# Fused relu-squared attention and GeGLU block: the last output tile on whole rows, one activation table, and a re-tuned instruction plan

## The chip, the cores and the metric

The kernel runs on 1 core of a Trainium2 chip. The metric is the device time of one execution in microseconds (us), lower is better. The kernel before takes 436.75 us, the median of 4 runs from 435.96 to 437.55.

## The reference

```python
def _attn_ref(q, k, v):                      # q, k, v: (8, 12, 448, 64) float32
    scores = (1 / np.sqrt(64)) * np.matmul(q, k.transpose(0, 1, 3, 2))
    attn = np.maximum(scores, 0.0) ** 2 / 448
    return np.matmul(attn, v)
...
x = attn_out.transpose(0, 2, 1, 3).reshape(3584, 768)
def _moe_ref(x, w_gate, w_val, w_out):       # (768, 1536), (768, 1536), (1536, 768)
    g = x @ w_gate
    gelu = 0.5 * g * (1.0 + erf(g / sqrt(2)))
    return (gelu * (x @ w_val)) @ w_out      # (3584, 768) float32
```

There is no softmax: the attention weight is the squared relu of a score. The output of attention, tokens by 768, goes straight through a gated feed-forward block.

## The kernel before, in words

All matrix products are in bf16 with 64x64 operands. TensorE's 128x128 array is used as four 64x64 quarters, two row halves ("lower" and "upper", after the input partitions 0 to 63 and 64 to 127) by two column halves; four matmuls on different quarters run side by side. A sum over 128 inputs is therefore made as two matmuls into the same PSUM bank: first the lower half's whole accumulation, then the upper half's. Two lists of operations, PE0 for the lower half and PE1 for the upper, are merged into TensorE's one instruction stream.

For each batch (b = 0 to 7) the work is:

- q, k and v are loaded by DMAs that GpSimd (POOL) issues, with a cast to bf16 (`load_qk`, `load_v`). Batches 0 and 1 come in three groups of four heads; batch 2 in one piece; from batch 3 on each load waits for a feed-forward step of the batch two before (`[done]` in `add_gate_value`), for batch 3 starting at step fc = 3 of batch 1.
- q and k are transposed into `qkT`. Batches 0 and 1 do it on TensorE (`add_transposes`: 28 small matmuls for a group, copied out by VectorE, L324); later batches copy q and k on VectorE into `qkr` (L249) and use seven DMA transposes from SyncE (L257).
- Scores (`add_scores`): 21 units a batch, each into one of two PSUM tiles `sp`; ScalarE takes the relu (`rl`, L367), VectorE squares it (`attnT`, L373).
- Values (`add_values`): the squares of a pair of heads times v give 128 rows of `xT` (VectorE copies and scales them, L422).
- Gate and value (`add_gate_value`): 12 steps fc; a gate accumulation goes through gelu on ScalarE (`gel`, L460), a value accumulation is multiplied with it on VectorE (`uT`, L465).
- Output (`add_out`): a tile of 128 tokens in two column groups of 384; each group is 12 lower and then 12 upper steps of two matmuls; ScalarE copies it out (`osb`, L512), and after the second group SyncE stores two times 64 rows (L517).

PSUM banks for everything but the scores come from a ring of four (`new_bank`, tag F).

The order of instructions on every engine is fixed when the program is built, by a planner. `work` holds every accumulation with a due time; `lower` and `upper` sort PE's operations; `run_plan` then plays the operations through with a cost and a lag for each and emits them as they would start. PE0 and POOL are queues in a fixed order; PE1, ACT, DVE and SP are pools from which the operation that can start first is taken. A load's arrival is played as its bytes over a rate (400 GB/s of float32) plus 2 us. Where PE would idle in the first 45 us of the plan, `fill` puts in dummy matmuls on zeros (`warm`, 128x128, 256 columns), which write nothing that is read. Each engine works its list strictly in order, so an operation that the plan places too early holds up all that is behind it.

Of the kernel before, what the change touches and what calls it, by code (L numbers as in the profile page):

```python
# [88 lines left out]
def kernel(  # L89
# [10 lines left out]
    nc = tc.nc  # L100
    f32 = mybir.dt.float32
# [42 lines left out]
    warm = const.tile([128, 512], bf16)  # L144
    nc.vector.memset(warm[:, :], 0.0)

    ctx.enter_context(tc.manual_schedule())

    HALF = (slice(0, P), slice(P, 2 * P))
# [20 lines left out]
    w12_op, wo_op, head_op = {}, {}, {}  # L170
    qk16, v16 = {}, {}

    def load(nbytes, emit, deps=(), cost=0.7):
        def paced():
            ins = emit()
            for d in deps:
                tc.add_manual_dep(ins.ins, d.ins.name, SYNC, reason="pace")

        op = Op("POOL", cost, paced, deps)
        arrivals[op] = nbytes / 400e3  # L180
        POOL.append(op)
        return op

# [14 lines left out]
    def load_qk(b, i, h0, h1, deps=()):  # L198

        src = (q, k)[i]  # L200

        def tile_of():
            if b not in qk16:
                qk16[b] = qkv.tile([128, H * S // P * D], bf16, name="qk16", tag="qk16")
            return qk16[b][HALF[i], :]

        op = load(4 * (h1 - h0) * S * D, lambda: nc.gpsimd.dma_start(  # L207
            tile_of().rearrange("p (h x) -> p h x", h=H)[:, h0:h1, :],
            src[b, h0:h1].rearrange("h (p c) d -> p h (c d)", c=SC)), deps)
        for pr in range(h0 // 2, h1 // 2):  # L210
            head_op[b, pr, i] = op

    def load_v(b, h0, h1, deps=()):

        for i in range(2):
            def emit(i=i):
                if b not in v16:
                    v16[b] = qkv.tile([128, H, VC, D], bf16, name="v16", tag="v16")
                c0 = i * (SC - VC)
                return nc.gpsimd.dma_start(  # L220
                    v16[b][HALF[i], h0:h1, :, :],
                    v[b, h0:h1].rearrange("h (p c) d -> p h c d", c=SC)[:, :, c0:c0 + VC, :])
            op = load(4 * (h1 - h0) * VC * P * D, emit, deps)
            for pr in range(h0 // 2, h1 // 2):
                head_op[b, pr, 2 + i] = op

# [81 lines left out]
    def add_transposes(at, b, m):  # L308

        box = {}  # L310

        def emit(i, pr, c):
            if i not in box:
                box[i] = new_bank(t_op[b, m, i], [128, 2, SC * P], bf16)
            t = box[i]
            src = qk16[b].rearrange("p (h c d) -> p h c d", c=SC, d=D)
            for j in range(2):
                nc.tensor.transpose(  # L318
                    t[HALF[j], pr, c * P:(c + 1) * P], src[HALF[i], 2 * (2 * m + pr) + j, c, :],
                    ident[HALF[i], HALF[i]], tile_position=(P * i, P * j))  # L320

        def emit_copy(i):
            dst = qkT_tile(b).rearrange("d (c r) x -> d r c x", c=SC)
            nc.vector.tensor_copy(  # L324
                dst[:, 2 * m:2 * m + 2, :, HALF[i]],
                box[i].rearrange("d r (c p) -> d r c p", c=SC))

        ops = [[], []]
        for i in range(2):
            have = [head_op[b, 2 * m, i], head_op[b, 2 * m + 1, i], *ring_dep()]  # L330
            for pr in range(2):
                for c in range(SC):
                    ops[i].append(Op(f"PE{i}", 0.05, lambda i=i, pr=pr, c=c: emit(i, pr, c),
                                     have, lag=0.2))
            t_op[b, m, i] = Op("DVE", 0.63, lambda i=i: emit_copy(i),
                               [ops[i][-1], last_s.get(b - 2)], lag=0.1, prio=1)
            DVE.append(t_op[b, m, i])
            ring.append(t_op[b, m, i])
        both(at, zip(*ops), GS / 2 if b else 0.0)

    def add_scores(at, b, u):
# [35 lines left out]
        else:  # L377
# [2 lines left out]
        ops = [[Op(f"PE{j}", 0.095 if tail else 0.189, lambda j=j, pr=pr: emit(j, pr), have, lag=0.24)  # L380
                for pr in prs] for j in range(2)]
        last_s[b] = ops[1][-1]
        relu = Op("ACT", 0.92, emit_relu, [ops[0][-1], ops[1][-1], *sq_list[-4:-3]], lag=0.06, prio=2)
        n_a = len(sq_list)
        sq = Op("DVE", 0.64, emit_sq, [relu, *att_free[n_a - 12:n_a - 11]] if n_a >= 12 else [relu],
                lag=0.1, prio=2)
        units.append(relu)
        sq_list.append(sq)
        att_free.append(None)
        for pr in prs:  # L390
            sq_op.setdefault((b, pr), []).append((sq, n_a))
        ACT.append(relu)
        DVE.append(sq)
        both(at, zip(*ops))

    sq_list, att_free = [], []

    def add_values(at, b, pr):
        box = {}
# [21 lines left out]
        def emit_copy():  # L421
            nc.vector.tensor_scalar_mul(xT[b][:, pr, :], box[0][:, 0:S], scalar1=out_scale)  # L422

        sqs = sq_op[b, pr]
        have = [*(s for s, _ in sqs), head_op[b, pr, 2], head_op[b, pr, 3]]
        order = ([0, 1, 2, 3], [3, 0, 1, 2])
        ops = [[Op(f"PE{i}", 0.189 if w < VC - 1 else 0.095, lambda i=i, w=w: emit(i, w),
                   [*have, *(ring_dep() if i == 0 else ())], lag=0.24) for w in order[i]]
               for i in range(2)]
        o_op[b, pr] = ops[1][-1]  # L430
        for _, n_a in sqs:
            att_free[n_a] = o_op[b, pr]
        x_op[b, pr] = Op("DVE", 0.63, emit_copy, [o_op[b, pr]], lag=0.1, prio=1)
        DVE.append(x_op[b, pr])
        ring.append(x_op[b, pr])
        then(at, 0.0, *ops, x_op[b, pr])
# [5 lines left out]
    def add_gate_value(at, b, fc, g):  # L442
# [28 lines left out]
        if g == 0:  # L471
            done = gel_op[b, fc] = Op("ACT", 0.55, emit_gelu, [ops[1][-1]], lag=0.06, prio=0)
            ACT.append(done)
        else:
            done = u_op[b, fc] = Op("DVE", 0.63, emit_mult, [gel_op[b, fc], ops[1][-1]],
                                    lag=0.1, prio=0)
            DVE.append(done)
            n = fc - (3 if b == 1 else 0)
            if b + 2 < B and b and 0 <= n < 9:
                h0 = 4 * (n % 3)  # L480
                if n < 6:
                    load_qk(b + 2, n // 3, h0, h0 + 4, [done])
                else:
                    load_v(b + 2, h0, h0 + 4, [done])
                if n == 5:
                    add_dma_transposes(b + 2)
        ring.append(done)
        then(at, GS, *ops, done)

    def add_out(at, t, g):  # L490

# [22 lines left out]
        def emit_store(j):  # L514
            b, c = chunks[j]
            rows = out[b * S:(b + 1) * S, :].rearrange("(p c) d -> c p d", c=SC)
            nc.sync.dma_start(rows[c], osb[t][HALF[j], :])  # L517

        ops = [[Op(f"PE{r}", RS, lambda r=r, fc=fc: emit(r, fc),
                   [wo_op[fc // WOG], *(u_op[b, fc] for b, _ in chunks),  # L520
                    *(ring_dep() if r == 0 and fc == 0 else ())], lag=0.24)
# [36 lines left out]
    for b in range(B):  # L558
        starts.append(at)
        for fc in range(FC):  # L560
            for g in range(2):
                work.append((at, 5, add_gate_value, (b, fc, g)))
                at += G

        while 2 * tile_no + 1 < SC * (b + 1) - (2 if b < B - 1 else 0):
            for g in range(NG):
                work.append((at, 5, add_out, (tile_no, g)))
                at += R
            tile_no += 1
    starts.append(at)  # L570
    LEAD = 6.0
    for b in range(B):
# [2 lines left out]
        elif b == 1:  # L575
            lo, hi = 0.0, starts[1] - LEAD
        elif b == 2:
            lo, hi = starts[1] + 6.0, starts[2] - LEAD
        else:
            lo, hi = starts[b - 1] - LEAD, starts[b] - LEAD  # L580
        step = (hi - lo) / NU
# [90 lines left out]
```

## Time and profile before

| what | value |
|---|---|
| median of 4 runs | 436.75 us (435.96 to 437.55) |
| the profiled execution | 436.18 us, its span 434.3 us |
| TensorE busy | 420.8 us, 97% |
| ScalarE, VectorE busy | 225.3 us (52%), 205.5 us (47%) |
| first real matmul | 4.98 us |
| first gate matmul | 31.43 us |
| last matmul ends, last copy ends, span ends | 429.3, 429.83, 434.3 us |
| activation tables loaded | two: at 0.74 us and at 34.27 us, 1.28 us each |
| dummy fill matmuls | 32 |
| stores | 56, issued by SyncE, 192 KB each |

A busy share of 97% says little by itself here, because a matmul on one quarter of the array counts as busy just like four on all quarters. What can be read is where TensorE's stream stands still, and what it stands for. A line of a timeline gives the start, the duration, the engine (PE for matmuls, PEld for their weight loads, DVE for VectorE, ACT for ScalarE, POOL for GpSimd, SP for SyncE), the source line, the operation, output<-inputs, and, in brackets, how long the engine idled before it and what ended that.

### The profile page before, as it was taken

What the parts mean: (1) busy time and instruction counts of PE and PEld (TensorE: products, weight loads), DVE (VectorE), ACT (ScalarE), POOL (GpSimd) and SP (SyncE); (2) the same over time, 40 slices, a digit from 0 to 9 for tenths busy, and PEclk for the clock granted to TensorE, in tenths of its full rate; (3) what the DMA queues carried; (4) which work ended last, traced back from release to release, by engine and by line L of the source; (5) the groups of instructions that cost most, each with busy time, mean ns of one, the idle gap of its engine ahead of it and who ended that gap; (6) DMA issues with size and microseconds to landing.
All of it is one profiled execution on the core that took longest, in us unless ns stands there. A gap on an engine that the chain in (4) does not pass through costs nothing.

```text
span 434.3 us, 19901 instructions
## 1 busy us (share of the span) xinstructions
PE 420.8 (97%) x9224; PEld 365.5 (84%) x9224; DVE 205.5 (47%) x367; ACT 225.3 (52%) x322; POOL 68.4 (16%) x110
## 2 busy tenths in 40 slices
PE   6999989999999999999999999999999999999995
PEld 3557968879988778999999878999999878977894
DVE  1885666156733565355733566345733555212200
ACT  1966654266655565465556555555546565322221
POOL 6654500012300230012200231012200000000000
PEclk8899999999999999999999999999999999999998
DMA  8999999916993679356943669346942100120034
GB/s 109 197 198 198 203 209 180 174 27 85 119 180 77 87 93 154 77 88 91 157 73 94 90 85 157 96 82 88 149 92 77 40 3 2 49 66 3 3 83 102
DMA packets 75154, 44.92 MB, mean 103 GB/s; under 512 B 36160, under 2 KB 71488, under 8 KB 75072
## 3 DMA queue, kind: packets, MB, share of 16 engines
q0 software_dynamic: 36992, 24.39, 41.3%
q1 hardware_dynamic: 38080, 19.28, 24.6%
q8 instruction: 72, 1.18, 1.1%
q14 instruction: 10, 0.08, 0.1%
HBM read 48.76 MB, written 11.01 MB: 138 GB/s over the span
## 4 chain that ended last, share of the span: by engine, by line
PE 83%; DMA 12%; POOL 2%; ACT 1%; issue 1%; DVE 0%; POOLq 0%; ACTq 0%; DVEq 0%
PE ff L155 77%; DMA qk<-in_k_dram 12%; PE sp L155 6%; POOL qk L207 1%; ACT rl L367 1%; POOL v L220 0%; ACT osb L512 0%; POOL wv L188 0%; PE ff L318 0%; DVE qkr L249 0%; DVE attnT L373 0%; DVE uT L465 0%; POOL ident masks.py:199 0%; POOL ident masks.py:197 0%; POOLq masks.py:199 0%
## 5 line engine op out<-in xcount | busy, mean ns | idle before, releaser
L155 PE MATMUL ff<-xT,wg 64*64 64x448 bf16 x2304 | 217.9, 349 | 0.2 <-issue 0.2
L155 PE MATMUL ff<-xT,wv 64*64 64x448 bf16 x2304 | 217.7, 349 | 0.0
L367 ACT ACTIVATE rl<-sp 128x896 bf16<-128x896 f32 x168 | 152.0, 923 | 107.3 <-PE sp L155 82.0
L155 PE MATMUL ff<-wo,uT 64*64 64x384 bf16 x2688 | 150.4, 323 | 1.0 <-DVE uT L465 1.0
L155 PEld LDWEIGHTS <-wg 64*64 64x64 bf16 x2304 | 130.2, 107 | 14.8 <-issue 0.6
L155 PEld LDWEIGHTS <-wv 64*64 64x64 bf16 x2304 | 130.2, 107 | 13.7 <-issue 1.0
L373 DVE TENSOR_TENSOR attnT<-rl 128x896 bf16<-128x896 bf16 x168 | 103.8, 623 | 78.9 <-ACT rl L367 77.8
L155 PEld LDWEIGHTS <-uT 64*64 64x64 bf16 x2688 | 126.2, 107 | 6.3 <-DVE uT L465 1.3
L155 PE MATMUL sp<-qkT 64*64 64x448 bf16 (+1 forms) x768 | 108.0, 333 | 2.5 <-ACT rl L367 1.1
L465 DVE TENSOR_TENSOR uT<-gel,ff 128x448 bf16<-128x448 bf16 x96 | 59.5, 620 | 79.3 <-PE ff L155 71.2
L155 PE MATMUL ff<-attnT,v 64*64 64x448 bf16 (+1 forms) x768 | 86.0, 326 | 0.0
L460 ACT ACTIVATE gel<-ff 128x448 bf16<-128x448 f32 x96 | 52.1, 543 | 51.2 <-PE ff L155 50.6
L155 PEld LDWEIGHTS <-qkT 64*64 64x64 bf16 x768 | 45.3, 107 | 12.7 <-issue 7.5
L512 ACT COPY osb<-ff 128x384 f32<-128x384 f32 x56 | 26.7, 476 | 45.3 <-PE ff L155 45.1
L155 PEld LDWEIGHTS <-v 64*64 64x64 bf16 x768 | 46.7, 107 | 3.5 <-issue 0.2
L422 DVE TENSOR_SCALAR xT<-ff 128x448 bf16<-128x448 f32 x48 | 29.9, 623 | 34.6 <-PE ff L155 33.5
L207 POOL DMA_DIRECT2D qk<-in_q_dram x22 | 13.9, 631 | 162.7 <-DVE uT L465 161.3
L220 POOL DMA_DIRECT2D v<-in_v_dram x44 | 27.5, 631 | 29.0 <-DVE uT L465 14.5
L207 POOL DMA_DIRECT2D qk<-in_k_dram x22 | 13.7, 622 | 33.6 <-DVE uT L465 32.5
L318 PEld LDWEIGHTS <-qk 64*64 64x64 bf16 x336 | 9.0, 116 | 6.7 <-DMA qk<-in_k_dram 4.4
L249 DVE COPY qkr<-qk 128x768 bf16<-128x768 bf16 x42 | 13.6, 363 | 1.7 <-DMA qk<-in_k_dram 1.7
L318 PE MATMUL ff<-ident,qk 64*64 64x64 bf16 x336 | 10.4, 201 | 3.7 <-DMA qk<-in_k_dram 2.7
(19 smaller groups left out, 38.9 us busy)
## 6 DMA issues: line engine op xcount, KB each, us to landing
out_dram<-osb SPq DMA_DIRECT2D x56, 192.0 KB, 2.7
v<-in_v_dram POOLq DMA_DIRECT2D x42, 128.0 KB, 4.9
qk<-in_q_dram POOLq DMA_DIRECT2D x21, 224.0 KB, 3.7
qk<-in_k_dram POOLq DMA_DIRECT2D x21, 224.0 KB, 3.8
wg<-in_moe_w_gate_dram POOLq DMA_DIRECT2D x6, 384.0 KB, 11.3
wv<-in_moe_w_val_dram POOLq DMA_DIRECT2D x6, 384.0 KB, 11.3
wo<-in_moe_w_out_dram POOLq DMA_DIRECT2D x4, 576.0 KB, 13.0
v<-in_v_dram POOLq DMA_DIRECT2D x2, 384.0 KB, 21.4
```

The source lines that it names most:

```text
L155: return nc.tensor.matmul(o, lhsT, rhs, start=start, stop=stop, tile_position=(P * row, P * col))
L207: op = load(4 * (h1 - h0) * S * D, lambda: nc.gpsimd.dma_start(tile_of().rearrange("p (h x) -> p h x", h=H)[:, h0:h1, :], src[b, h0:h1].re ...
L220: return nc.gpsimd.dma_start(v16[b][HALF[i], h0:h1, :, :], v[b, h0:h1].rearrange("h (p c) d -> p h c d", c=SC)[:, :, c0:c0 + VC, :])
L249: nc.vector.tensor_copy(box[0][:, c], qk16[b].rearrange("p (h c d) -> p c h d", c=SC, d=D)[:, c])
L318: nc.tensor.transpose(t[HALF[j], pr, c * P:(c + 1) * P], src[HALF[i], 2 * (2 * m + pr) + j, c, :], ident[HALF[i], HALF[i]], tile_position= ...
L367: nc.scalar.activation(rl[:, :, :], box[0][:, :, 0:S], AF.Relu)
L373: nc.vector.tensor_tensor(a[:, :, :], box[1][:, :, :], box[1][:, :, :], op=ALU.mult)
L422: nc.vector.tensor_scalar_mul(xT[b][:, pr, :], box[0][:, 0:S], scalar1=out_scale)
L460: nc.scalar.activation(gel[b, fc][:, :], box[0][:, 0:S], AF.Gelu)
L465: u_op[b, fc].ins = nc.vector.tensor_tensor(uT[b][:, fc, :], gel.pop((b, fc))[:, :], box[0][:, 0:S], op=ALU.mult).ins
L512: nc.scalar.copy(ob[:, cols], box[0][:, 0:OGS])
```

## The change

The changed kernel does six things:

1. A one-column gelu on ScalarE ahead of everything loads the table of gelu first; the relus and copies then use the same table.
2. Batch 0's loads are planned at 300 GB/s in place of 400.
3. The planner's costs for VectorE and ScalarE operations are smaller by 0.09 to 0.12 us and their lags larger by the same amount (0.63 and 0.1 become 0.54 and 0.2).
4. In the plan each step of a value accumulation waits for the square that it reads and not for all squares of the pair; for odd pairs the order of the lower steps changes.
5. Batch 3's loads start at step fc = 0 of batch 1 in place of 3, and batch 2's scores are due 4 us later.
6. The last output tile uses matmuls over all 128 input rows (two 128x64 halves of the array), in three column groups of 384, 192 and 192. Each group is copied out and stored when it is done, one half of the rows from SyncE's queue, the other from ScalarE's.

```diff
+    nc.scalar.activation(warm[:, 0:1], warm[:, 1:2], AF.Gelu)
...
-    def load(nbytes, emit, deps=(), cost=0.7):
+    def load(nbytes, emit, deps=(), cost=0.7, rate=400e3):
...
-        arrivals[op] = nbytes / 400e3
+        arrivals[op] = nbytes / rate
...
-            src[b, h0:h1].rearrange("h (p c) d -> p h (c d)", c=SC)), deps)
+            src[b, h0:h1].rearrange("h (p c) d -> p h (c d)", c=SC)), deps, rate=400e3 if b else 300e3)
...
-        relu = Op("ACT", 0.92, emit_relu, [ops[0][-1], ops[1][-1], *sq_list[-4:-3]], lag=0.06, prio=2)
+        relu = Op("ACT", 0.8, emit_relu, [ops[0][-1], ops[1][-1], *sq_list[-4:-3]], lag=0.18, prio=2)
...
-        have = [*(s for s, _ in sqs), head_op[b, pr, 2], head_op[b, pr, 3]]
-        order = ([0, 1, 2, 3], [3, 0, 1, 2])
+        have = [head_op[b, pr, 2], head_op[b, pr, 3]]
+        order = ([0, 3, 1, 2] if pr % 2 else [0, 1, 2, 3], [3, 0, 1, 2])
...
-                   [*have, *(ring_dep() if i == 0 else ())], lag=0.24) for w in order[i]]
+                   [*have, sq_of[b, pr, w], *(ring_dep() if i == 0 else ())], lag=0.24)
+                for w in order[i]]
...
-            n = fc - (3 if b == 1 else 0)
-            if b + 2 < B and b and 0 <= n < 9:
-                h0 = 4 * (n % 3)
+            if b + 2 < B and b and fc < 9:
+                h0 = 4 * (fc % 3)
...
+    def add_last_out(at, t, g, chunks):
+        box = {}
+        cols = slice(*((0, OGS), (OGS, OGS + OGS // 2), (OGS + OGS // 2, 2 * OGS))[g])
+        n = cols.stop - cols.start
+        def emit(fc):
+            if not box:
+                box[0] = new_bank(cp)
+            for j, (b, c) in enumerate(chunks):
+                nc.tensor.matmul(box[0][HALF[j], 0:n], uT[b][:, fc, c * P:(c + 1) * P],
+                                 wo[fc // WOG][:, fc % WOG, cols], start=fc == 0, stop=fc == FC - 1,
+                                 tile_position=(0, P * j))
+        def emit_copy():
+            if g == 0:
+                osb[t] = opool.tile([TT, d_model], f32, name="osb", tag="osb")
+            nc.scalar.copy(osb[t][:, cols], box[0][:, 0:n])
+        def emit_store(j):
+            b, c = chunks[j]
+            rows = out[b * S:(b + 1) * S, :].rearrange("(p c) d -> c p d", c=SC)
+            (nc.sync, nc.scalar)[j].dma_start(rows[c, :, cols], osb[t][HALF[j], cols])
+        cost = RS * n / OGS
+        los = [Op("PE0", cost, lambda fc=fc: emit(fc),
+                  [wo_op[fc // WOG], *(u_op[b, fc] for b, _ in chunks), *(ring_dep() if fc == 0 else ())],
+                  lag=0.24) for fc in range(FC)]
+        his = [Op("PE1", cost, lambda: None, [lo]) for lo in los]
+        cp = Op("ACT", 0.48, emit_copy, [los[-1]], prio=1)
+        ring.append(cp)
+        ACT.append(cp)
+        SP.append(Op("SP", 0.6, lambda: emit_store(0), [cp], prio=-1))
+        ACT.append(Op("ACT", 0.1, lambda: emit_store(1), [cp], prio=-1))
+        both(at, zip(los, his))
...
+        if 2 * t + 2 == B * SC:
+            add_last_out(at, t, g, chunks)
+            return
...
-            for g in range(NG):
+            for g in range(NG + (2 * tile_no + 2 == B * SC)):
...
-            lo, hi = starts[1] + 6.0, starts[2] - LEAD
+            lo, hi = starts[1] + 10.0, starts[2] - LEAD
```

## The prediction

> **What bounds the kernel now.** I read the page's busy shares, then the chain of work that ended last, then TensorE's timeline wherever its stream stands still, and for each such place the timeline of the engine that it waits for.
>
> ```profile
> PE 420.8 (97%) x9224; PEld 365.5 (84%) x9224; DVE 205.5 (47%) x367; ACT 225.3 (52%) x322; POOL 68.4 (16%) x110
> PE 83%; DMA 12%; POOL 2%; ACT 1%; issue 1%; DVE 0%; POOLq 0%; ACTq 0%; DVEq 0%
> ```
>
> TensorE is the bound, and the DMA part of the chain lies in the first 72 us, where loads come in at 196 to 212 GB/s in every stretch of 5 us from 15 to 70 us. From 75 to 110 us and from 130 to 400 us matmuls cover the time (35.00 of 35.00 and 269.65 of 270.00 us), so a gain must come from the few places where the stream stops. After 35 us I find these of 0.5 us or more:
>
> ```profile
> 39.23 0.38 PE L155 MATMUL ff<-xT,wg 64*64 64x448 bf16 x2
> 39.97 0.28 PE L318 MATMUL ff<-ident,qk 64*64 64x64 bf16 x6 [0.36 <-DMA qk<-in_k_dram]
> ...
> 72.28 0.33 PE L155 MATMUL ff<-wo,uT 64*64 64x384 bf16 x2
> 73.56 0.76 PE L155 MATMUL ff<-wo,uT 64*64 64x384 bf16 x8 [0.95 <-DVE uT L465]
> ...
> 125.23 0.38 PE L155 MATMUL ff<-attnT,v 64*64 64x448 bf16 x2
> 126.26 0.38 PE L155 MATMUL sp<-qkT 64*64 64x448 bf16 x4 [0.65 <-ACT osb L512]
> ```
>
> A 448-column step takes 0.19 us in the gate (starts 38.48, 38.66, 38.85) and a 384-column step 0.16 (71.96, 72.12, 72.28). So the stream stops for 0.55 us at 39.97, 1.12 at 73.56, 0.84 at 126.26. The last is put down to a copy, but that copy ends at 125.94; the last DMA transpose of batch 3 lands at 126.06, and TensorE has its own wait for those semaphores until 126.16. Two more stops, 1.0 us at 55.48 and 0.5 at 57.71, wait for "issue" (no wait shows) and for a VectorE copy; the order around them is the same in the changed program, so I keep them.
>
> **The plan's part of the change.** The built order of both programs tells what moves.
>
> At 39.97 batch 1's second group of k transposes waits for its load, which lands at 39.93. In the changed order 16 more gate matmuls stand ahead of them, four full steps of 0.19, 0.75 us. That covers the stop of 0.55 and lets up to 0.2 us of any earlier gain through: I take **-0.7** (0 if the q half, landed at 38.80, stops it instead; at most -0.9). The same landing swallows what is saved ahead of it. So I cost at nothing: the second table load that goes (1.28 us at 34.27), the steps that wait for their own square, and the other fills (25 in place of 32, with the granted clock at 0.74 from 5 to 10 us and 0.58 from 10 to 15). If that landing were no cover, the table load alone would be worth up to 1.28 us. The new gelu delays the warm-up matmuls, behind which all of TensorE's list stands: from 1.19 to about 2.3 us (the table load ends at 2.02, then a one-column operation, estimated 0.2 from the copy's 0.48 for 384 columns and the relu's 0.92 for 896). Warm-up takes 3.7, the q transposes 0.63, three fills 0.33: 7.0 us, and k's transposes wait for their load until 7.73 anyway. The cover has 0.7 us left.
>
> At 73.56 VectorE's list decides:
>
> ```profile
> 69.23 0.62 DVE L465 TENSOR_TENSOR uT<-gel,ff 128x448 bf16<-128x448 bf16 x1 [0.25 <-PE ff L155]
> 71.55 0.36 DVE L249 COPY qkr<-qk 128x768 bf16<-128x768 bf16 x1 [1.69 <-DMA qk<-in_k_dram]
> ...
> 72.89 0.62 DVE L465 TENSOR_TENSOR uT<-gel,ff 128x448 bf16<-128x448 bf16 x1
> ```
>
> The copies of batch 2's q and k stand ahead of batch 0's last product, and their load lands only at 71.45. In the changed order (arrivals planned later) all seven copies stand behind that product. Its inputs end at 71.58; with 0.62 and a hand-over of 0.1 it is there at 72.3, when TensorE wants it. The stop goes: **-1.1** (0 to -1.1). Late next are batch 1's last xT and batch 2's transposes, but those feed scores that now start 84 gate matmuls later (768 against 684).
>
> At 126.26 batch 3's loads start three gate steps earlier, some 8 us by the spacing of the load issues (93.41, 96.05, 98.70), so its transposes land about 7 us before they are wanted: **-0.8** (0 to -1.0). SyncE's list then has batch 2's transposes split three and four by a pair of stores that wait for a copy, at worst some us late, covered by the later scores. Scores that stop for 0.28 us near 144.1, 243.4 and 342.8 move by a few instructions: 0 (to -0.8 for all three). Sum of the plan: **-2.6**.
>
> **The last tile.** At the end the upper half of the last group runs alone:
>
> ```profile
> 426.76 0.25 PE L155 MATMUL sp<-warm 64*64 64x64 bf16 x4
> 427.01 2.30 PE L155 MATMUL ff<-wo,uT 64*64 64x384 bf16 x26
> 429.35 0.48 ACT L512 COPY osb<-ff 128x384 f32<-128x384 f32 x1 [1.10 <-PE ff L155]
> ```
>
> Whole-row matmuls should remove this lone half. But in the built order the upper half of the group before (tile 26's second) is scattered among them, and its last two steps still stand at the very end, behind the filler. From the first step of the last tile on, the old stream has 37 steps of 0.16 (12 + 12 + 13); the new one 12 + 12 whole steps (half of the latter as twice as many of half length) and 14 lone upper steps, 38: **+0.16**. The lone half is not removed, it is cut into pieces; and between the pieces the array changes from 128-row matmuls to 64-row ones and back **26 times**. Before has no such change in its tail, but its fills (128x128) show one:
>
> ```profile
> 16.50 0.35 PE L155 MATMUL sp<-qkT 64*64 64x448 bf16 x2
> 16.78 0.50 PE L285 MATMUL ff<-warm 128*128 128x256 bf16 x3
> 17.21 0.38 PE L155 MATMUL sp<-qkT 64*64 64x448 bf16 x4
> 17.53 0.50 PE L285 MATMUL ff<-warm 128*128 128x256 bf16 x3
> 17.96 0.38 PE L155 MATMUL sp<-qkT 64*64 64x448 bf16 x4
> ```
>
> From 17.21 to 17.96 are 0.75 us; one step of 0.19 and three fills of 0.11 (256 columns at the same pace) leave 0.23 for two changes, **0.115 each**; 16.50 to 16.78 less 0.19 gives 0.09. Bounds for a change between 128x64 and 64x64, which no row shows undisturbed: 0, if only the row half counts, and 0.21, the idle time of the weight loads at each change:
>
> ```profile
> 17.21 0.11 PEld L155 LDWEIGHTS <-qkT 64*64 64x64 bf16 x4 [0.21 <-issue]
> ```
>
> I take the nearest, 0.115: 26 x 0.115 = **+3.0** (0 to +5.5).
>
> The Trainium skill speaks against this edit: "TensorEngine Tiling (Array Packing)", section Key Properties, says that a change of tiling mode, not merely of the tile, drains TensorE. It gives no price; by that rule the sum has 26 drains, and without it none.
>
> Stores: the last copy again is tile 26's, with its two 192 KB stores from SyncE (issue 0.47 and 0.59, the second from 430.37, landing at 433.08), so the end behind it stays. New ahead of it on ScalarE are the copy of the last 192 columns (0.32, from the copy's 0.48 less 192 columns at the relu's slope) and a store's issue (0.47 as on SyncE; 0.1 if ScalarE only hands it over, 0.6 at most), together 0.8, against 0.57 for the filler and two steps on TensorE: **+0.25** (0 to +0.4). Two queues save nothing where the last store isn't theirs.
>
> Another place where page and trace differ costs nothing either way: "ScalarE: Activation LUTs", section What ACT_TABLE_LOAD costs, adds a drain of about 1.38 us to the load's 1.28. Here gelu starts at 35.56, right behind the load of 34.27 to 35.55; by the page the removal would be worth up to 2.7 us, by the row 1.28, and both lie behind the landing at 39.93.
>
> **Sum.** 436.18 - 2.6 + 0.16 + 3.0 + 0.25 = 436.99 on the profiled execution, which lies 0.57 below the median of the runs; on the median it would be 437.56. I forecast **437.2**, with 0.2 for that. About 0.3% (1.3 us) is what a measurement of this kernel can tell from no change: 435.44 to 438.06.
>
> **Rivals.**
> A, the change of rows is free: -2.6 + 0.41 gives 433.99, with the 0.2 **434.2**, faster. For it: between 128x64 and 64x64 the column halves stay. Against it: the gap of 0.09 in both directions. It decides below 0.048 a change.
> B, slower, one mechanism: at each of the 26 changes the weights cannot be loaded ahead, so that the whole 0.21 of the weight-load row is paid: 5.46 + 0.41 - 2.6 gives 439.45, **439.7**. It decides from 0.149 a change on. Against it: matmuls hide part of this time in the fills.
> C, the plan's gains don't come: TensorE, 0.7 us early after 39.97, stands for another landing or for instruction issue (as at 55.48), and only the 0.8 at 126.26 stays: 436.18 - 0.8 + 3.41 = 438.79, **439.0**, slower. For it: loads run without pause until 75 us. Against it: the order behind 39.97 shows no load that lands later than it is wanted.
> That the last tile doesn't do what it says, leaving a lone half at the end, is in the forecast already.
>
> **Chances.** Forecast 0.42, A 0.22, B 0.16, C 0.20: faster 0.22, same 0.42, slower 0.36. The range reaches from just below A to B, 433.9 to 439.8; what it leaves out is several plan gains failing under B's price, or the 0.8 of the small stops under A.
>
> **What would show it.** Right: no stop above 0.2 us near 40, 73 and 126 us; one table load; in the last 9 us 26 gaps of about 0.1 between rows of 128x64 and 64x64, the last matmul two lone steps after the filler, ScalarE's last copy waiting on its own queue. Wrong: whole and half steps at 0.16 without gaps (A), gaps of 0.2 (B), or a new stop between 40 and 125 us (C).

## The result and the profile after

The changed kernel took **437.27 us** (median of 53 runs, 435.95 to 439.26), the kernel before 436.32 in the runs beside it (79 runs, 435.14 to 439.94). The ratio is **1.0014, 95% interval 1.0005 to 1.0023**: 0.2 to 1.0 us slower, well within the 0.3% that the prediction set as its bound for "no change". The profiled execution took 436.57 us with a span of 434.8, against 436.18 and 434.3.

Behind this small number stand two large ones of opposite sign. They show first in the page's busy shares and in its chain of work:

```profile
PE 421.5 (97%) x9193; PEld 353.9 (81%) x9193; DVE 205.6 (47%) x367; ACT 224.4 (52%) x323; POOL 68.3 (16%) x110
PE 92%; DVE 4%; ACT 2%; issue 1%; ACTq 0%
```

The 12% of DMA in the chain are gone, TensorE has 31 matmuls fewer and is busy 0.7 us longer. Busy time alone thus says nothing of what was won: pauses between two matmuls of a busy stream count as busy in part. I therefore add up, from the trace, the matmul work that is real (no filler), each matmul at its columns times 0.16 us per 384 columns and at its share of the array, and call the time that remains **lost**. The real work is the same in every kernel here, so the difference of two kernels' lost time, up to some point, is what one is ahead there.

| up to | before, lost us | after, lost us | difference |
| --- | --- | --- | --- |
| 40 us | 23.53 | 22.11 | -1.42 |
| 50 us | 24.24 | 23.59 | -0.65 |
| 70 us | 27.09 | 26.20 | -0.89 |
| 75 us | 28.69 | 26.76 | -1.93 |
| 125 us | 30.15 | 28.41 | -1.74 |
| 135 us | 31.43 | 28.61 | -2.82 |
| 420 us | 40.16 | 37.44 | -2.72 |
| time of the last matmul's start | 428.99 | 429.26 | +0.28 |
| time of the span's end | 434.33 | 434.80 | +0.47 |

So the plan won 2.7 us by 135 us, kept them to 420, and the last tile gave 3.0 back on TensorE (from -2.72 to +0.28) and 0.19 behind it. These are TensorE's rows where the last tile begins, from the timeline of the changed kernel:

```profile
420.20 0.35 PE L503 MATMUL ff<-wo,uT 128*64 128x384 bf16 x2
420.48 0.11 PEld L157 LDWEIGHTS <-uT 64*64 64x64 bf16 x2 [0.17 <-issue]
420.48 0.35 PE L157 MATMUL ff<-wo,uT 64*64 64x384 bf16 x2
...
420.76 0.35 PE L503 MATMUL ff<-wo,uT 128*64 128x384 bf16 x2
```

L503 is a whole-row step of the last tile, L157 a lone upper step of tile 26. Steps of 0.16 start 0.28 apart: at each change of the rows TensorE pauses for 0.12. The weight load's own gap, 0.17 in place of 0.21 in the fills before, starts while the last matmul still runs and is no price.

The end, from the same timeline:

```profile
429.17 0.32 ACT L510 COPY osb<-ff 128x192 f32<-128x192 f32 x1 [1.87 <-PE ff L503]
429.26 0.33 PE L157 MATMUL ff<-wo,uT 64*64 64x384 bf16 x2
...
429.52 0.50 ACTq L515 DMA_DIRECT2D out_dram<-osb  x1
430.06 0.48 ACT L551 COPY osb<-ff 128x384 f32<-128x384 f32 x1 [0.57 <-PE ff L157]
430.56 1.11 SPq L556 DMA_DIRECT2D out_dram<-osb  x2
```

The last copy is put down to PE, but TensorE's last step ended at 429.59. What it really waits for is the row above: ScalarE issues a store from 429.52 to 430.02, and does nothing else meanwhile.

### The profile page after: what moved, and what is told of

It reads as the page before. It is cut to its first block, busy times and chain, and to the rows that moved or that the text cites. A ratio compares the mean times of both kernels' runs of the same rounds, so it can differ in the third digit from the quotient of the medians.

```text
span 434.8 us, 19846 instructions
## 1 busy us (share of the span) xinstructions
PE 421.5 (97%) x9193; PEld 353.9 (81%) x9193; DVE 205.6 (47%) x367; ACT 224.4 (52%) x323; POOL 68.3 (16%) x110
## 3 DMA queue, kind: packets, MB, share of 16 engines
q1 hardware_dynamic: 38160, 19.08, 24.6%
## 4 chain that ended last, share of the span: by engine, by line
PE 92%; DVE 4%; ACT 2%; issue 1%; ACTq 0%
PE ff L157 82%; PE sp L157 7%; ACT rl L369 2%; DVE attnT L375 2%; PE ff L503 1%; DVE qkT L326 1%; PE ff L678 1%; DVE xT L425 1%; PE ff L320 0%; ACT L147 0%; DVE uT L469 0%; ACTq L515 0%; ACT osb L551 0%; PE ff L287 0%; ACT osb L510 0%
## 5 line engine op out<-in xcount | busy, mean ns | idle before, releaser
L157 PE MATMUL ff<-xT,wg 64*64 64x448 bf16 x2304 | 215.9, 349 | 0.0
L157 PE MATMUL ff<-xT,wv 64*64 64x448 bf16 x2304 | 213.6, 349 | 0.7 <-DVE uT L469 0.7
L157 PE MATMUL ff<-wo,uT 64*64 64x384 bf16 x2592 | 149.4, 323 | 0.1
L157 PEld LDWEIGHTS <-wv 64*64 64x64 bf16 x2304 | 123.7, 107 | 18.2 <-issue 2.5
L157 PEld LDWEIGHTS <-wg 64*64 64x64 bf16 x2304 | 124.4, 107 | 16.6
L157 PEld LDWEIGHTS <-uT 64*64 64x64 bf16 x2592 | 118.7, 107 | 9.2 <-issue 1.9
L157 PE MATMUL sp<-qkT 64*64 64x448 bf16 (+1 forms) x768 | 106.5, 328 | 3.2 <-ACT rl L369 2.3
L157 PE MATMUL ff<-attnT,v 64*64 64x448 bf16 (+1 forms) x768 | 85.8, 326 | 0.8 <-DVE attnT L375 0.7
L157 PEld LDWEIGHTS <-qkT 64*64 64x64 bf16 x768 | 44.0, 106 | 14.0 <-issue 5.4
L157 PEld LDWEIGHTS <-v 64*64 64x64 bf16 x768 | 45.0, 107 | 6.0 <-issue 1.7
L551 ACT COPY osb<-ff 128x384 f32<-128x384 f32 x54 | 25.7, 476 | 41.0 <-PE ff L157 41.0
```

Of the source, the lines that this page charges most:

```text
L157: return nc.tensor.matmul(o, lhsT, rhs, start=start, stop=stop, tile_position=(P * row, P * col))
L551: nc.scalar.copy(ob[:, cols], box[0][:, 0:OGS])
```

## The experiments

The theory that the prediction left: the plan is worth about -2.7, the last tile about +3.3, nearly all of it 26 pauses of 0.115. Rivals: the plan's gain does not reach the end; the pauses are free, and the cost is in the shape of the whole-row steps or in the order of the last stores.

### The plan alone and the last tile alone

`plan_only` is the changed kernel without the new tile:

```
-        if 2 * t + 2 == B * SC:
-            add_last_out(at, t, g, chunks)
-            return
-            for g in range(NG + (2 * tile_no + 2 == B * SC)):
+            for g in range(NG):
```

> The changed kernel with the last tile as it was (one group of 384 columns after the other, each half on its own rows, both stores from SyncE); the plan's edits and the early gelu stay. My theory (plan worth -2.6, last tile worth +3.4 to +3.6): no change of rows is left in the tail, so 2.6 to 2.7 us below the kernel before, about 433.6, a ratio near 0.994. Rival, the plan's gains do not reach the end and the last tile costs next to nothing: within 0.5 us of the kernel before, a ratio of 0.999 to 1.001. In the trace by my theory: no stop of over 0.3 us at 126 us, and the last 28 steps behind the filler as before, 2.3 us at the pace of 0.16.

Measured: 434.03 us, ratio **0.9945 (0.9923 to 0.9966)**, -2.4 us of 436.55. `tail_only` adds the same lines, and `add_last_out`, to the kernel before:

> The kernel before with only the last tile of the change (whole rows, three column groups, stores from two queues). My theory (0.115 us at each change between 128 and 64 rows, 28 such changes in its built order where the changed kernel has 26; one step more; 0.44 us of ScalarE's store ahead of the last copy): 28 x 0.115 + 0.16 + 0.44 = 3.8 us above the kernel before, about 440.1, a ratio near 1.0088. Rival A, a change of rows is free: +0.6, ratio 1.001. Rival B, a change costs the whole 0.21 of the weight load's row: +6.5, ratio 1.015.

Measured: 439.86 us, ratio **1.0092 (1.0063 to 1.0120)**. The profiled execution, the slowest of the six, was already 3.2 us behind the kernel before at 415 us (granted clock 0.5 from 9.3 to 22.9 us), so only its last part can be read: from 415 us to the last matmul it loses 3.1 us more than the kernel before, and from there to the end it takes 5.53 against 5.34. The built order had 26 changes, not the 28 that I had counted into the expectation. Both halves of the theory hold; a plan that gains nothing and a free change of rows are out.

### The same steps with 2, 6 and 26 changes of rows

`tail_block` is the changed kernel with the lone upper steps kept together ahead of the last tile (a place holder in the lower list pairs with them):

```
+        if g == 0:
+            for _ in range(2):
+                lower.append((at - 1e-6, Op("PE0", 0.3, lambda: None)))
+            los[0].deps.append(last_up[-1])
...
+        if 2 * t + 4 == B * SC and g == NG - 1:
+            last_up.extend(ops[1])
```

> The changed kernel, but the twelve lone upper steps of tile 26 all stand ahead of the last tile, so that its 24 + 24 whole-row matmuls run in one piece: the same steps and instructions, 2 changes of rows in place of 26, and the end is the last tile's own 192 columns with one store of each queue. My theory: 24 x 0.115 = 2.8 us less than the changed kernel from the changes, and at the end a copy of 0.32 in place of 0.48 and one store per queue in place of two in a row, 0.5 to 1.1 less: 3.3 to 3.9 less than the changed kernel, about 433.6, a ratio to the kernel before near 0.994. Rival A, the changes are free and the cost lies in the whole-row matmuls themselves (more and shorter instructions): only the end's 0.5 to 1.1 comes, a ratio near 1.000. In the trace by my theory: whole-row steps of 384 columns 0.16 apart, of 192 columns 0.08, without the pause of 0.115.

Measured: 433.24 us, ratio **0.9930 (0.9905 to 0.9955)**, below both kernels. TensorE's part of its tail:

```profile
422.45 4.12 PE L505 MATMUL ff<-wo,uT 128*64 128x384 bf16 x72
```

72 whole-row matmuls of 384 and 192 columns in one piece, two side by side. At the pace of the row-half steps (0.1625 us for 384 columns, 0.0813 for 192) they make 12 x 0.1625 + 24 x 0.0813 = 3.9 us, and the distance from 422.45 to the filler at 426.50, less 0.1 for the change there, is 3.95. Whole-row steps themselves cost nothing beyond their columns, within 0.05 us.

By the traces the span is 3.8 us shorter than that of the changed kernel: 2.9 up to the start of the last matmul, where the changes are, and 0.9 behind it (4.62 against 5.53), where the last copy and stores are smaller. Against `plan_only` the two intervals overlap, so these runs do not show that whole rows gain anything over the old last tile. By the two traces TensorE gains nothing in the tail (its last matmul starts 0.57 sooner, all of it won before 420 us), and the end gains 0.7 (4.62 against 5.34).

`tail_pieces` puts the twelve steps in four pieces of three:

```
-            los[0].deps.append(last_up[-1])
+        los[0].deps.append(last_up[3 * g + 2])
+        last_up[3 * g + 3].deps.append(los[-1])
```

> The changed kernel with tile 26's twelve lone upper steps in four pieces of three between the column groups of the last tile: 6 changes of rows in place of 26, and, as in the changed kernel, the last copy and stores are tile 26's (two of 192 KB, one after the other from SyncE). If the price is paid per change, 0.115 each as read from the trace: 20 fewer changes, 2.3 us less than the changed kernel, and up to 0.4 more since six lone steps (0.96) and the filler now cover ScalarE's 192-column copy and store ahead of the last copy: about 434.0, between the block of the last experiments (ratio 0.993) and the changed kernel (1.001), near 0.9945 to 0.9955. Rival, the price is paid once for a tail with mixed rows, however many changes it has: equal to the changed kernel. Rival, it was the order of the end (last stores) that made the block faster: no more than 0.5 below the changed kernel.

Measured: 434.42 us, ratio **0.9963 (0.9950 to 0.9976)**, between the two. A lone piece, a whole-row piece and the next lone piece in its timeline:

```profile
423.24 0.68 PE L157 MATMUL ff<-wo,uT 64*64 64x384 bf16 x6
...
423.85 1.18 PE L505 MATMUL ff<-wo,uT 128*64 128x192 bf16 x24
...
424.96 0.68 PE L157 MATMUL ff<-wo,uT 64*64 64x384 bf16 x6
```

Three lone steps are 0.49 us; 423.24 to 423.85 is 0.61: a pause of 0.12. Twelve pairs of 0.08 are 0.98 (0.0813 each); 423.85 to 424.96 is 1.11: 0.13, of which 0.10 fall on the change. Taken over all starts, the distance of two steps less the time of the first one's columns:

| kernel | changes | 64 to 128 rows, median | 128 to 64, median | sum |
| --- | --- | --- | --- | --- |
| after | 26 | 0.120 | 0.099 | 2.92 |
| tail_only | 26 | 0.120 | 0.099 | 2.94 |
| tail_pieces | 6 | 0.096 | 0.099 | 0.61 |
| tail_block | 2 | 0.123 | 0.099 | 0.22 |

The price goes by the number of changes: 0.10 to 0.12 each, 0.112 on the mean of 26. Pieces are 2.3 us cheaper than the changed kernel by this table, and 0.14 by their end (5.39 from the last matmul against 5.53), together a ratio of 0.9958; my expectation of up to 0.4 at the end was too high, since only three lone steps, and not six, follow the last whole-row piece: ScalarE's copy and store still hold the last copy until 0.68 behind the last matmul's start (0.80 in the changed kernel).

### The end: three column groups and two queues

`tail_halves` has the plan, the three column groups and the two queues, but row halves as before, so no change of rows:

```
+        last = 2 * t + 2 == B * SC
+        H0 = OGS // 2
+        cols = (slice(*((0, OGS), (OGS, OGS + H0), (OGS + H0, 2 * OGS))[g]) if last
+                else slice(g * OGS, (g + 1) * OGS))
...
+            if last:
+                (nc.sync, nc.scalar)[j].dma_start(rows[c, :, cols], osb[t][HALF[j], cols])
+                return
```

> The plan of the change with the last tile on separate row halves as before, but in the three column groups of 384, 192 and 192 with stores from SyncE and ScalarE: the groups and the two queues without a single change of rows. My theory: the plan's -2.7 stays whole; the lone half that runs at the end is 192 columns wide, and a copy of 0.32 and one store per queue follow it: 0.5 to 1.1 below the kernel with the plan alone, about 432.8, a ratio to the kernel before near 0.992. Rival, two queues bring nothing since the landing of a store (2.7 us from issue here) sets the end whatever its size: the same as the plan alone within 0.2 us.

Measured: 434.12 us, ratio 0.9947 (0.9927 to 0.9966): the same as the plan alone. By the trace the end is 0.39 shorter (4.95 from the last matmul's start against 5.34), less than the 0.5 to 1.1 that I expected, because of this:

```profile
427.27 0.32 ACT L520 COPY osb<-ff 128x192 f32<-128x192 f32 x1 [0.62 <-PE ff L157]
427.61 0.50 ACTq L526 DMA_DIRECT2D out_dram<-osb  x1
428.15 0.32 ACT L520 COPY osb<-ff 128x192 f32<-128x192 f32 x1 [0.57 <-ACT osb L520]
```

TensorE ended at 426.99; the last copy starts 1.16 later, behind a copy and a store on its own engine. An effect of 0.4 us is below what these runs can tell, so it stands on one trace. Five of the twelve runs had a mean granted clock of 0.988 and took 435.0 to 435.8 us; the other seven, at 0.996 and above like all of `plan_only`, have a median of 433.46 against its 434.03, which points the same way.

In `tail_block` a store held ScalarE even longer, 1.23 us. `block_sync` gives it only the very last store:

```
-            (nc.sync, nc.scalar)[j].dma_start(rows[c, :, cols], osb[t][HALF[j], cols])
+            (nc.sync, nc.scalar if g == 2 else nc.sync)[j].dma_start(rows[c, :, cols], osb[t][HALF[j], cols])
```

> The block of the last experiments (lone upper steps together ahead of the last tile) with the stores of the first two column groups both from SyncE, so that only the last 48 KB store is issued by ScalarE. In the block's trace ScalarE's second store held the engine for 1.23 us, and the last copy started at 427.40 although its matmuls end near 426.6. My theory: the last copy starts 0.7 to 0.8 earlier; SyncE's own store of the last group is now queued behind four others (the second pair took 1.24 in the block) and is issued near 427.4: 0.3 to 0.7 less than the block, ratio to the kernel before near 0.992. Rival, the landing of the pair of 96 KB stores sets the end whoever issues them: the same as the block.

Measured: 434.07 us, ratio 0.9946 (0.9929 to 0.9963). The expectation failed. The last copy did start early (427.82, the last whole-row step ending at 427.77), but the delay had moved to SyncE: its second store took 1.46 us, and its last one was issued at 429.74, 1.9 us after that copy began; from the last matmul's start to the end 5.17 us against 4.62. Relative to `tail_block` the two intervals overlap, and this execution also stood 0.6 at 90 us (below).

`after_sync` is the changed kernel with all stores from SyncE (their operations move to SyncE's list in the plan as well):

```
-            (nc.sync, nc.scalar)[j].dma_start(rows[c, :, cols], osb[t][HALF[j], cols])
+            nc.sync.dma_start(rows[c, :, cols], osb[t][HALF[j], cols])
```

> The changed kernel with every store from SyncE; in its built order the last 192-column store of the last tile then stands behind tile 26's two stores. My theory: ScalarE's last copy no longer waits for its own store (0.44 us in the changed kernel) and starts at once after TensorE's last step, but SyncE has three stores to issue one after the other behind it (0.47, 0.59 and 0.55) where there were two: from TensorE's last step to the end 5.2 to 5.6 us against 5.53, no gain of over 0.3, ratio to the changed kernel 0.9995. Rival, two queues are what shortens the end: 0.5 or more above the changed kernel.

Measured: 437.38 us against 437.27 of the changed kernel, a ratio to the kernel before of 1.0034 (1.0004 to 1.0064), which overlaps that of the changed kernel. The profiled execution, 441.19 us, is the slowest of twelve for a reason that comes below. The end of its trace:

```profile
434.06 0.33 PE L157 MATMUL ff<-wo,uT 64*64 64x384 bf16 x2
434.42 0.48 ACT L551 COPY osb<-ff 128x384 f32<-128x384 f32 x1
434.93 1.13 SPq L556 DMA_DIRECT2D out_dram<-osb  x2
436.11 0.59 SPq L515 DMA_DIRECT2D out_dram<-osb  x1
```

Without the store the last copy starts 0.36 after TensorE's last step started (0.80 in the changed kernel), and the third store of SyncE takes most of that back: 5.36 from the last matmul to the end, as expected. The Trainium skill's page "Trainium Kernel Development and Optimization", section Key Constraints, says that issuing DMAs from several engines only saves the issue time of the sequencer; here not even that comes free, as the issue holds the engine that makes the copies for 0.50 us.

### The plan's parts

`rate_only` is the kernel before with one edit, the 300 GB/s for batch 0's loads:

```
+    def load(nbytes, emit, deps=(), cost=0.7, rate=400e3):
+        arrivals[op] = nbytes / rate
+            src[b, h0:h1].rearrange("h (p c) d -> p h (c d)", c=SC)), deps, rate=400e3 if b else 300e3)
...
+            op = load(4 * (h1 - h0) * VC * P * D, emit, deps, rate=400e3 if b else 300e3)
```

> The kernel before with one of the plan's edits: batch 0's loads planned at 300 GB/s, so that the copies of batch 2's q and k stand one place later in VectorE's list, behind batch 0's last product. My theory: the stop of 1.12 us near 73.5 goes, and nothing else of that size: 1.0 to 1.1 less than the kernel before, ratio 0.9975. Rival, the copies are late anyway and the next landing takes the time back: no change. In the trace also: a stop of about 1.2 us that waits for 'issue' came at the 1982nd TensorE load or matmul in every kernel so far whatever stood there (before, the changed one and four variants); this kernel has twenty more of these instructions early on, so if the stop belongs to the instruction's number it is at the 1982nd again, if to the work that stands there it moves to about the 2002nd.

Measured: 439.36 us, ratio **1.0068 (1.0047 to 1.0090)**, slower. The stop at 73 us went, as expected: from 70 to 75 us the kernel loses 0.50 us, the kernel before 1.60. But a stop of the rival's kind came, larger than the gain:

```profile
85.24 1.11 PE L155 MATMUL ff<-xT,wv 64*64 64x448 bf16 x14
88.17 0.38 PE L155 MATMUL sp<-qkT 64*64 64x448 bf16 x4 [1.82 <-DMA qkT<-qkr]
```

These are batch 2's first scores; the copies that the edit moved behind batch 0's last product feed SyncE's DMA transposes, which now land after the scores want them. That execution took 437.61 us, the least of the four; what the others, at 439.3 to 439.7, lost besides is not traced. `rate_starts` adds the edit that plans those scores later:

```
-            lo, hi = starts[1] + 6.0, starts[2] - LEAD
+            lo, hi = starts[1] + 10.0, starts[2] - LEAD
```

> The kernel before with two of the plan's edits: batch 0's loads planned at 300 GB/s, and batch 2's transposes and first scores planned 4 us later, which in the built order moves those scores 80 half-array matmuls further back. With the first edit alone TensorE stood 1.8 us at 86 us for the DMA transposes of batch 2, whose copies that edit had moved back, and took more than the whole gain back. My theory: 80 x 0.095 = 7.6 us of other matmuls now cover that landing; no stop at 73 us and none at 86: 1.0 to 1.1 less than the kernel before by those two, and about the 0.8 of the fuller clock at the start, in all 1.0 to 1.9 less, ratio 0.9955 to 0.998. Rival, VectorE's late copies put off batch 2 whatever the plan: the stop moves some us back and stays, ratio 1.003 to 1.007.

Measured: 435.23 us, ratio **0.9979 (0.9957 to 1.0000)**, 0.9 less than the kernel before. In its trace there is no stop at 73 and none at 86, and the lost time at 420 us is 38.80 against 40.16, 1.4 less. So the gain at 73 needs both edits: one moves the wait away from TensorE, the other makes room for it. Not all of the 0.9 is that gain: the two kernels' traces differ by 1.1 between 70 and 75 us and by 0.3 more up to 135.

`loads_only` starts batch 3's loads three gate steps earlier:

```
-            n = fc - (3 if b == 1 else 0)
+            n = fc
```

> The kernel before with one of the plan's edits: batch 3's loads start at gate step 0 in place of 3. My theory: its transposes land some 7 us earlier and the stop of 0.84 us at 126.26 goes, 0.8 less than the kernel before, ratio 0.998. Rival, another wait of the same scores (their q and k copies, the ring of buffers) stands just behind: the stop stays above 0.4 us.

Measured: 435.64 us, ratio 0.9993 (0.9979 to 1.0008), which does not tell it from no change. The trace does, at the place: from 125 to 130 us the kernel loses 0.11 us, the kernel before 0.88, and these scores stand among other matmuls without a wait:

```profile
125.53 0.41 PE L155 MATMUL sp<-qkT 64*64 64x448 bf16 x4
...
125.88 1.88 PE L155 MATMUL ff<-wo,uT 64*64 64x384 bf16 x40
```

The early gelu I tried from both sides. `table_only` adds its one line to the kernel before, `no_gelu` takes it from the changed kernel:

```
+    nc.scalar.activation(warm[:, 0:1], warm[:, 1:2], AF.Gelu)
```

> The kernel before with the early gelu alone: one table load in place of two, the warm-up matmuls from 2.3 in place of 1.2. As the prediction had it the 1.28 us of the second load lie behind the landing at 39.9: no change, ratio 0.9985 to 1.0015. Rival from the traces since: where TensorE stood idle for over 1.1 us between the warm-up and 11 us, its granted clock fell to 0.5 for 3 to 9 us (the kernel before: idle 2.13 to 7.74, half from 7.4 to 14.2; the loads edit alone: idle 2.16 to 11.08, half from 11.5 to 14.5); the later warm-up shortens that idle time by 1.1 us, the clock stays full and up to 0.9 us of lost matmul time by 15 us go; these then either reach the end (ratio 0.998) or stop at the landing near 39.9 (1.000).

> The changed kernel without the early gelu: two table loads again, the warm-up from 1.2. If the table's 1.28 us count (no landing stops TensorE at 40 us in the changed order any more, it waits there for ScalarE's relu by way of VectorE): up to 1.3 us above the changed kernel, ratio to the kernel before near 1.004, with a stop of 1 to 2 us between 34 and 42 us. If they lie under matmuls: equal to the changed kernel, 1.001. Besides, the fill that the plan places behind k's transposes and the idle time in front of them (from about 5.9 to 7.3) tell whether the clock holds without the delay of the warm-up: a half-clock stretch would add about 0.9.

Measured: 436.39 us, ratio 1.0002 (0.9979 to 1.0026), and 436.76 us, ratio 1.0007 (0.9993 to 1.0022), against 1.0014 of the changed kernel. No change on either side. `table_only` shows where a gain can go: at 75 us it had lost 0.7 us less than the kernel before, and at 135 us only 0.2 less, since it then stood 1.6 us (start to start) for batch 3's transposes in place of 1.0. In `no_gelu` the second table load is there, and TensorE does not feel it (lost time at 35 us 21.28, in the changed kernel 21.42):

```profile
33.09 1.28 ACT L462 ACT_TABLE_LOAD   x1
34.38 0.54 ACT L462 ACTIVATE gel<-ff 128x448 bf16<-128x448 f32 x1
```

## Why the prediction was right, step by step

As a ratio to the kernel before the forecast was 1.0010 (437.2 to 436.75); measured 1.0014. Both large terms were found by runs of their own, the plan at -2.4 (-3.4 to -1.5) and the last tile at +4.0 (2.7 to 5.2). That the time itself came within 0.1 us of the forecast is luck: the errors of the single terms are larger, and the kernel before measured 0.4 less than in its first four runs.

**The last tile.** Forecast +3.41 for the profiled execution (0.16 + 3.0 + 0.25), measured +3.2 (3.0 on TensorE, 0.19 behind it). The price of a change, 0.115 from the fills' rows, measured 0.112 (0.120 into the whole rows, 0.099 back). The three groups of rows with 2, 6 and 26 changes put rival A (free, below 0.048) and rival B's price (0.21) out. Rival B's mechanism is not out. In the lines of the changed kernel above, the weight load at a change starts together with its matmul (both at 420.48), whereas inside a piece of one shape, as in that of `tail_block`, the loads of 384-column steps run 0.16 ahead of their matmuls; and the pause of 0.10 to 0.12 is about as long as one load, 0.11. Whether it is this load that cannot run ahead, or the array that has to empty, no run here separates. The step that decided was to read the built order, in which the lone half is scattered, instead of the diff, which says that whole rows replace it.

**The end.** Forecast +0.25, measured +0.19. The mechanism is right and both sides of it were mis-sized: the last copy was later by 0.44 (0.80 in place of 0.36 behind the last matmul's start), since copy and store with their hand-overs held ScalarE for 0.89 (429.17 to 430.06) and the filler and two steps covered only 0.45 of it; and 0.22 came back behind the last landing, which no step had: from there to the span's end it is 1.27 us in the kernel before and 1.04 in the changed one. It is 1.27 to 1.29 in the six traces with the old last tile and 1.02 to 1.08 in the eight with three column groups, those with stores from SyncE alone or with row halves included. Why was not tried.

**The stop at 126 us.** Forecast -0.8; -1.1 between 125 and 135 us in the changed kernel, and -0.8 from the loads edit by itself. Right, and by the mechanism given: the changed kernel's scores at that place stand among other matmuls without a wait.

```profile
125.60 0.35 PE L157 MATMUL sp<-qkT 64*64 64x448 bf16 x2
125.66 0.62 PE L157 MATMUL ff<-wo,uT 64*64 64x384 bf16 x8
125.98 0.38 PE L157 MATMUL sp<-qkT 64*64 64x448 bf16 x2
```

**The stop at 73 us.** Forecast -1.1, measured -1.04 between 70 and 75 us. Right, with the step that made it hold: that batch 2's transposes would be late next, but feed scores that come 84 matmuls later. `rate_only` is the case without that step, and it is rival C. The changed kernel runs through the place in one piece:

```profile
71.42 3.34 PE L157 MATMUL ff<-wo,uT 64*64 64x384 bf16 x70
```

I put the pair of stores that splits these transposes at "at worst some us late, covered by the later scores". That was too sure. The cover is thin: these are SyncE's rows of the changed kernel, and of `after_sync`, which has the same order up to here.

```profile
72.88 4.71 SPq L259 DMA_TRANSPOSE qkT<-qkr  x3
77.63 1.23 SPq L556 DMA_DIRECT2D out_dram<-osb  x2
78.91 5.74 SPq L259 DMA_TRANSPOSE qkT<-qkr  x4
```

```profile
73.95 5.18 SPq L259 DMA_TRANSPOSE qkT<-qkr  x3
79.17 2.49 SPq L556 DMA_DIRECT2D out_dram<-osb  x2
81.71 6.35 SPq L259 DMA_TRANSPOSE qkT<-qkr  x4
```

The store pair took 2.49 in place of 1.23, the last four transposes ended 3.4 us later (1.1 of it from the start), and TensorE stood for them for 2.05 us at 92; in `block_sync` for 0.6 at 90.

```profile
92.12 0.38 PE L157 MATMUL sp<-qkT 64*64 64x448 bf16 x2 [2.05 <-DMA qkT<-qkr]
```

In `after_sync` the stop cost twice its length, since the granted clock then fell to 0.5 from 93.4 to 96.8: from 89 to 125 us it lost 5.2 us, the changed kernel 1.2. In the six other profiled executions of this plan TensorE did not stand there. So rival C does live in the changed kernel's plan, in some executions.

**The stop at 40 us.** Forecast -0.7, measured -0.65 by 50 us in this trace; the mechanism was wrong in its main part, and that the sizes agree is luck. I had TensorE 0.7 ahead because its stop for the load would go, and all gains ahead of 40 us swallowed by a landing that I took to stay at 39.93. In the changed kernel that load landed at 39.48 and stopped nothing. It was 1.4 us ahead at 40, 0.9 of it already at 15 us, where its granted clock is 1.00 and the kernel before had 0.5 from 7.4 to 14.2. Then a new stop took back about 0.8:

```profile
41.25 0.38 PE L157 MATMUL ff<-xT,wv 64*64 64x448 bf16 x2 [0.72 <-DVE uT L469]
```

VectorE's list shows why; the square ahead of the product waits for a relu that ended at 40.01:

```profile
40.04 0.62 DVE L375 TENSOR_TENSOR attnT<-rl 128x896 bf16<-128x896 bf16 x1 [1.45 <-ACT rl L369]
40.59 0.61 DVE L469 TENSOR_TENSOR uT<-gel,ff 128x448 bf16<-128x448 bf16 x1
```

"No stop above 0.2 us near 40" was thus wrong. It is also the least stable term: over eight profiled executions of this plan the lost time at 50 us runs from 23.6 to 24.6 (mean 24.1), the kernel before having 24.2, and at 70 us from 26.2 to 27.4, the kernel before having 27.1. It goes with the moment at which the trace first grants the full clock, from 4.5 us in `no_gelu` and 5.9 in the changed kernel to 8.1 in `plan_only`: until then the warm-up matmuls of 512 columns start 0.43 apart, and 0.22 afterwards. Over all of them but `after_sync`, with its stop at 92, the mean at 420 us is 37.8, so the plan is worth 2.4, as the runs of `plan_only` have it, rather than the 2.7 of one trace. Of these 2.4 their means put 0.4 ahead of 70 us, where the forecast had 0.7, 1.1 between 70 and 75, and 1.0 between 125 and 135; the rest nearly cancels.

**The table load** at nothing was right from both sides, and the small stops near 144, 243 and 342 us (0 expected) brought nothing: from 135 to 405 us both kernels lose 8.4 us.

## What to carry to other kernels

A change between 64-row and 128-row matmuls has a price for each change (0.10 to 0.12 us here, with 384 and with 192 columns): gather the steps of one shape, and count the changes in the built order, since a planner that fills holes scatters what the code writes as a block. With the same plan, the same twelve lone steps and the same last tile, in one piece, made the kernel 0.7% faster than before, scattered 0.14% slower; the plan without the new tile made it 0.55% faster. An edit that takes a wait away by moving work back only gains if what that work feeds is moved back too; and a second store queue on the engine that makes the copies costs its issue time there.

## What was not expected of the hardware

**A stop that belongs to an instruction's number.** In all fourteen kernels profiled here TensorE stands 0.85 to 1.5 us (start to start) ahead of its matmul number 991, counted from 0 in the order of the trace, and the trace names no wait. In the changed kernel, and in `rate_only`, which has ten more matmuls ahead of it than the kernel before, so that other transposes stand there:

```profile
54.98 0.28 PE L320 MATMUL ff<-ident,qk 64*64 64x64 bf16 x7 [1.00 <-issue]
```

```profile
55.23 0.26 PE L318 MATMUL ff<-ident,qk 64*64 64x64 bf16 x9 [0.66 <-issue]
```

In the DMA part of the trace a queue of kind "instruction" moves one packet of 0.02 MB in that stretch in both. But each of the kernels has 72 such packets, one every 6 us or so, and no other matmul number behind the warm-up has a stop above 0.22 us in all fourteen. That this stop is the loading of instructions, held up by the other loads, was not tried.

**The clock behind a pause.** The granted clock fell to 0.5 in four executions while there was work left. Three have the order of the kernel before, at the start: that kernel itself from 7.4 to 14.2 us, around an idle time of 2.13 us; `loads_only` from 11.5 to 14.9, behind one of 2.16; and `tail_only` from 9.3 to 22.9, behind one of 1.15. The fourth is `after_sync`, from 93.4 to 96.8, behind its stop of 2.05. These stretches last 6.83, 3.41, 13.65 and 3.41 us, whole multiples of 3.41. The Trainium skill, "TensorE: Matmul & The Clock Gate", section Part 1: The HAM clock gate, gives an idle window of about 3.4 us ahead of half clock; here less was enough. But `table_only` kept the full clock through 1.6 us of idle time at 13 us, and behind the last matmul, where nothing follows, it fell after 0.8 us of idle time in one execution and after 4.2 in another. So no fixed length of a pause decides; what does is open.

**DMA issues of uneven length.** A store's issue took 0.47 to 0.60 us as a rule, and 1.2 to 1.9 in 27 of 816 (all profiled kernels together), one of them on ScalarE: in `tail_block`, where SyncE's was held at the same moment (426.13 to 427.37). What holds them is open.
